# Four edits to a fused attention and Fourier-mixing kernel: spare products, raw weight places, two copies, the list of steps

## The chip, the cores and the metric

The kernel runs on one core of a Trainium2 chip. The metric is the device time of one execution in microseconds (us), lower being better; runs are given as a median with the lowest and the highest. The engines are TensorE (PE in the profile, with its weight loads as PEld), VectorE (DVE), ScalarE (ACT), GpSimd (POOL) and SyncE (SP), which issues most of the transfers. Each engine works through its own instructions in the order in which the program lists them.

## What is computed

For 4 batches of 8 heads, 768 tokens and head size 48, a gated linear attention; then, on the heads laid side by side (768 tokens by 384), a Fourier mixing block. Everything is f32.

```python
f = 1.0 / (1.0 + np.exp(-f_logit))
for t in range(S):
    state = f[:, :, t, :, None] * state + np.einsum('bhd,bhe->bhde', k[:, :, t], v[:, :, t])
    y[:, :, t] = np.einsum('bhd,bhde->bhe', q[:, :, t], state)
...
mixed = np.real(np.fft.fft(np.fft.fft(x, axis=1), axis=2))
u = x + mixed
un = (u - mean(u)) / np.sqrt(var(u) + 1e-06)
out = u + np.maximum(un @ w_ch1, 0.0) @ w_ch2
```

w_ch1 is 384 by 1536 and w_ch2 is 1536 by 384. They arrive as 64-bit floats, two 32-bit words per number, and the kernel makes f32 of them.

## The kernel before

**The order is written by hand.** The string ORDER holds 720 words; the kernel walks through them, and each word issues the next piece of one activity to the engines' queues. Nothing reorders the instructions afterwards, so the list sets the order on every engine, SP's and POOL's queues included.

- A number (0 to 15) is the next step of that attention unit. A unit is a pair of heads of one batch: units 0 to 3 are batch 0. Its steps, in order: exp and ln on ACT (L372, L373); a scan over the tokens on DVE (L379); three exps on ACT (L383, L384, L387); two multiplies on DVE (L391, L392); the score products on PE (L400); a masked copy on DVE (L404); products with v into the PSUM tile y (L559), the second score products (L576) and their copy to ao on ACT (L579); the rest of L559 and the state products (L599); a scan of the states on DVE (L607); the products of q with the states (L616) into y and five copies to yT on ACT (L625 to L629); transposes on PE (L636) and two copies to x on ACT (L640, L641); the fold of the tokens on DVE (L663 to L669); for units 2 and 3 of a batch also the sums over the channels (L678 to L687). There is one tile y, so the next unit's L559 waits for the yT copies of the one before it. K is the transpose of the keys (L538) and its copy to kT (L540).
- F is the next step of a batch's Fourier part: four z products (L725) with copies on ACT (L728 to L730), then three mix products (L744), whose sums go to x on DVE (L800, L803) with mean and variance (L766, L767). The first z needs the folds of all four units of the batch. H normalises a block of 128 tokens (L780), transposes it (L783) and copies it (L784).
- P is the next step of a batch's products with w_ch1 and w_ch2. Batch 0 goes through plain products (L872 up, L881 down); later batches use sums of blocks that save products (L841 up, L895 down). B makes one of the sums of w_ch1 (L813, L815), W the sums of w_ch2 (L358 to L361, in combine).
- C makes f32 of one block of weights (128 by 384): ACT scales the low words (L281), DVE shifts and masks the high words (L283, L284), POOL adds the two (L285). There are 24 blocks. r is the load of one block's raw words (L310) and R of three; V loads raw words again later and c looks at their sizes (L344).
- L loads the f, k, q or v of a unit (L206 to L213). I and Z set constants on POOL (I also the tile bound, which every scan reads), T and S load and sort the Fourier tables, i loads the identity, M joins the flags that decide whether a second, careful pass is needed.
- D is a group of spare products (L192): eight bf16 products of 128 by 128 of the tile bound with itself, into an unused part of y. Nobody reads them. There are 21 groups, all before F0.

**The raw words** lie in a pool tile with three places. A place is free again when POOL's addition (L285) of its block is done. The sums of w_ch2 (t2, t3, t4 in combine) use the same three places afterwards.

**The fold.** In L663 to L669 DVE makes sums and differences of mirrored tokens. Two of its seven instructions are plain copies: L667, f[:, 1:7:5] from f[:, 0:8:7] (128 x 192), and L668, one row f[0:1, 0] from f[0:1, 2] (1 x 96). The last one, L669, writes f[0:1, 2] and f[0:1, 6] and so must come after L668.

Of the kernel before, what the change touches and what calls it, by code (L numbers as in the profile page):

```python
# [7 lines left out]
F32 = mybir.dt.float32  # L8
U32 = mybir.dt.uint32
# [3 lines left out]
C = 128  # L13
# [11 lines left out]


ORDER = (
    "I L0f D L1f 0 D 0 1 L2f D D D D D L0q L0k D L1k 2 Z 0 D 1 i D D L1q L3q 0 0 0 L0v L3fk D 1 r 1 L2q D "
    "D L1v L2k 2 0 1 K0 3 0 0 D r 3 r D 2 0 1 1 2 C K1 L2v 1 2 1 C 3 2 C 1 K2 3 L4fk 4 2 r 1 2 L5fk D 4 5 "
    "L3v 1 3 2 D D T C 2 3 0 L4qv K3 5 3 0 2 3 D 3 2 3 S 2 3 D 3 L6fk 6 R 3 4 F0 5 F0 4 L5qv F0 C F0 5 "  # L30
    "L6qv K4 C r C 4 4 r F0 5 4 H0 H0 r C 4 H0 4 C L7fk r F0 r 7 F0 6 4 P0 C L7qv K5 P0 P0 r C r 5 C P0 r "
    "7 P0 5 6 4 6 P0 C C P0 5 K6 5 L8fk r C P0 7 7 P0 5 6 r P0 C 8 P0 r 6 r C P0 6 7 C K7 H0 C r 7 P0 r 6 "
    "C r 6 5 P0 C 6 H0 C P0 B 7 r C 6 r C 7 H0 L9fk L8qv P0 8 P0 P0 9 9 7 9 L9qv 6 P0 P0 P0 P0 9 7 9 K9 "
    "H0 P0 8 9 P0 P0 7 5 P0 P0 B P0 P0 8 7 B 9 8 4 9 H0 B W P0 P0 P0 9 P0 6 P0 P0 L11fk B P0 11 P0 P0 P0 "
    "P0 B B P0 11 9 8 K8 7 P0 P0 P0 11 8 F1 F1 F1 P0 P0 B L11qv F1 B P0 8 11 8 F1 11 8 L10fk P0 H1 B 10 B "
    "K11 P0 P0 P0 P0 L10qv 10 B 10 P0 10 P0 P0 10 H1 11 P0 P0 10 B B P0 B P0 H1 B P0 10 K10 P1 P1 P1 P1 "
    "P1 P1 P1 P1 L12fk P1 P1 P1 P1 P1 P1 F1 P1 F1 10 8 12 10 P1 8 12 10 12 9 P1 P1 P1 P1 L12qv 12 11 9 12 "
    "P1 H1 P1 H1 P1 12 11 K12 H1 H1 11 11 H1 L13fk P1 P1 P1 L13qv P1 P1 P1 P1 P1 P1 13 P1 P1 P1 P1 P1 13 "
    "P1 P1 12 10 P1 P1 13 13 12 10 12 11 P1 P1 P1 11 10 P1 L14fk 14 12 P1 K13 P1 11 F2 F2 P1 P1 14 P1 P1 "
    "L14qv P1 F2 P1 P1 14 P1 P1 P1 P1 P1 P1 14 F2 13 F2 P1 13 F2 P1 13 F2 P1 13 14 L15fk H2 15 13 14 13 "  # L40
    "K14 P1 15 L15qv 15 P1 P1 P1 14 15 H2 P1 H2 14 H2 P1 P2 14 P2 P2 P2 P2 P2 P2 P2 P2 P2 P2 P2 P2 P2 P2 "
    "13 14 15 K15 H2 H2 15 15 14 P2 V 15 H2 14 15 13 P2 14 c V 15 12 12 P2 P2 15 P2 15 V P2 P2 15 P2 F3 "
    "F3 F3 P2 H2 c V P2 P2 P2 V V P2 P2 P2 P2 P2 P2 P2 c P2 c c F3 P2 V F3 V F3 V c P2 P2 F3 P2 P2 P2 P2 "
    "P2 P2 H3 P2 H3 P2 V P2 P2 H3 P2 c P2 c c P2 P2 V P2 P2 P2 P2 P2 P2 P2 V P2 P2 P2 c c P2 c V V c V P2 "
    "V P2 P2 V P2 P2 H3 P3 c H3 P3 P3 P3 P3 P3 P3 P3 P3 P3 P3 P3 P3 c P2 P3 P3 H3 c P3 P3 P3 V P3 V P3 V "
    "c P3 P3 H3 P3 P3 H3 P3 c V P3 P3 P3 P3 P3 P3 P3 P3 V P3 P3 P3 P3 c P3 c P3 P3 P3 P3 P3 P3 P3 P3 P3 "
    "P3 V P3 c c P3 P3 P3 P3 P3 P3 c V P3 c P3 P3 P3 P3 P3 M P3 P3 P3 P3 P3 P3 P3 P3"
)


# [33 lines left out]
def kernel(  # L84
# [13 lines left out]
    nc = tc.nc  # L98
    B, HP, _, D, _, S = qkf.shape
    NCH = S // C  # L100
    DM = HP * 2 * D
    DFF = w_ch1.shape[1]
    NF = DFF // 128
    NQ = S // 4 + 1
    HS = S // 2
    HD = DM // 2
    QS, QD = S // 4, DM // 4
    R = 64 + D
# [9 lines left out]
    pr = ctx.enter_context(tc.tile_pool(name="pr", bufs=3))  # L118
# [7 lines left out]
    spare = y_out[:, 0, 3 * C:]  # L126

    def fixed(shape, tag):
        return const.tile(shape, F32, tag=tag, name=tag)
# [20 lines left out]
    bound = const.tile([128, S], mybir.dt.bfloat16, tag="bound", name="bound")  # L150
# [13 lines left out]
    eps = fixed([128, 1], "eps")  # L164
    two = fixed([128, 1], "two")
    small = fixed([128, 2 * NF], "small")

    place = const.tile([128, B, 4], U32, tag="place", name="place")

# [17 lines left out]
    started = []  # L187

    def busy():

        for _ in range(8):
            nc.tensor.matmul(spare, lhsT=bound[:, :C], rhs=bound[:, :C], start=not started, stop=True,  # L192
                             skip_group_check=True)
            started.append(True)

    v_of = {}
# [108 lines left out]

    def words(i):
        _, src, cols = blocks_of[i]
        raw = pr.tile([128, 2, 3, DM // 2], U32, tag="raw", name=f"raw{i}").rearrange("p a b n -> p (a b n)")
        raw = raw[:, :768].rearrange("p (n w) -> p n w", w=2)
        nc.sync.dma_start(out=raw.rearrange("p n w -> p (n w)"),  # L310
                          in_=src.bitcast(U32)[:, 2 * cols.start:2 * cols.stop])
        return raw

    def fetch(n=1):
        for _ in range(n):
            if wide and len(raws) < len(blocks_of):
                raws.append(words(len(raws)))
# [32 lines left out]
    def combine():  # L350

        H = NF // 2
        w11, w12, w21, w22 = [w2[:, i * H:(i + 1) * H, j * HD:(j + 1) * HD] for i in range(2) for j in range(2)]
        t2, t3, t4 = [pr.tile([128, H, HD], F32, tag="raw", name=f"block{i}") for i in range(3)]
        tt = nc.vector.tensor_tensor
        tt(t3, w22, w12, ALU.subtract)  # L358
        tt(w12, w12, w11, ALU.subtract)
        tt(t2, w22, w12, ALU.subtract)  # L360
        tt(t4, w21, t2, ALU.subtract)  # L361
        blocks[1], blocks[2], blocks[4] = w11, w21, t4
        blocks[5], blocks[6], blocks[3], blocks[7] = w12, t2, w22, t3
# [178 lines left out]
    def outputs(u, x_all, AT, Q, K, te, T=None):  # L542
# [98 lines left out]
        nc.scalar.copy(x_to[:, 3:], heads[:, 3:])  # L641
        yield
        yield from fold(u, x)

    eo_of = {}

    def fold(u, x):

        b, hp = divmod(u, HP)
        if b not in eo_of:
            eo_of[b] = p1.tile([128, 8, DM], F32, tag="eo", name=f"eo{b}")
        eo = eo_of[b]
        ch = slice(hp * 2 * D, (hp + 1) * 2 * D)
        f = eo[:, :, ch]  # L660
        last = hp == HP - 1
        tt = nc.vector.tensor_tensor
        tt(f[:, 6:3:-1], x[:, 0:3, ch], x[:, 3:6, ch], ALU.subtract)  # L663
        tt(f[:, 1:4], x[:, 0:3, ch], x[:, 3:6, ch], ALU.add)
        tt(f[:, 0:8:7], f[:, 1:7:5], f[:, 2:6:3], ALU.add)
        tt(f[:, 2:6:3], f[:, 1:7:5], f[:, 2:6:3], ALU.subtract)
        nc.vector.tensor_copy(f[:, 1:7:5], f[:, 0:8:7])  # L667
        nc.vector.tensor_copy(f[0:1, 0], f[0:1, 2])  # L668
        tt(f[0:1, 2:7:4], x[0:1, 0:2, ch], x[0:1, 3:5, ch], ALU.subtract)  # L669
        if hp < HP // 2:  # L670
            return
        yield


        lo, hi = (QD + 1, HD) if hp == HP // 2 else (1, QD + 1)
        up = slice(DM - lo, DM - hi, -1)
        tt = nc.vector.tensor_tensor
        tt(xs[:, :, lo:hi], eo[:, 4:7, lo:hi], eo[:, 4:7, up], ALU.subtract)  # L678
        if last:
            eo_of.pop(b)  # L680
            tt(se[:, :, 1:QD], xs[:, :, 1:QD], xs[:, :, HD - 1:QD:-1], ALU.subtract)
            tt(xs[:, :, 1:QD + 1], xs[:, :, 1:QD + 1], xs[:, :, HD - 1:QD - 1:-1], ALU.add)
        tt(xc[:, :, lo:hi], eo[:, 0:4, lo:hi], eo[:, 0:4, up], ALU.add)
        if last:
            nc.vector.tensor_copy(xc[:, :, 0:HD + 1:HD], eo[:, 0:4, 0:HD + 1:HD])
            tt(ce, xc[:, :, 0:QD + 1], xc[:, :, HD:QD - 1:-1], ALU.add)
            tt(xc[:, :, 0:QD], xc[:, :, 0:QD], xc[:, :, HD:QD:-1], ALU.subtract)  # L687
# [269 lines left out]
    with tc.manual_schedule():  # L957
        for word in ORDER.split():
            kind, n = word[0], int("0" + "".join(c for c in word if c.isdigit()))
# [10 lines left out]
            elif kind == "P":  # L970
                next(rest[n], None)
            elif kind == "W":
                combine()
            elif kind == "B":
                weight_sum()
# [31 lines left out]
    with tc.If(again > 0):  # L1007
        if wide:
            for i, (dst, _, _) in enumerate(blocks_of):
                single_or_zero(dst, words(i))  # L1010
        else:
            for i, (dst, src, cols) in enumerate(blocks_of):
                nc.sync.dma_start(out=dst, in_=src[:, cols])
        combine()
        nc.sync.dma_start(out=causal.rearrange("p (i n) -> p i n", n=32), in_=sel)
        for u in range(4):
            load(u, *("fkqv" if u < 3 else "qv"))
        for b in range(B):
            x = p2.tile([128, NCH, DM], F32, tag="x", name=f"again{b}")
            for hp in range(HP):  # L1020
                for _ in attention_by_blocks(b * HP + hp, lambda: x):
                    pass
            for _ in fnet(b, x):
                pass
            for _ in projected(b, x, again=True):
                pass
# [69 lines left out]
```

## Time and profile before

| | |
|---|---|
| median of 3 runs | 528.33 us (527.76 to 528.81) |
| the profiled execution | 527.43 us |
| its span, first to last instruction | 525.7 us |
| mean granted TensorE clock | 0.98 |
| busy PE / PEld / DVE / ACT / POOL | 94% / 86% / 72% / 41% / 12% |
| chain that ended last | PE 80%, DVE 9%, DMA 4%, issue 2%, ACT 2% |
| moved by DMA | 48.15 MB, mean 92 GB/s |

The busy shares are averages over the whole span. In the lines shown further on, a line of the timeline or of the chain begins with the start in us and the duration in us; behind it come engine, line of the kernel, operation, and what is written from what. A square bracket at the end gives how long the engine stood idle before the instruction and what released it. Where a line ends in x24, so many instructions are merged. An f32 product written once in the program shows as two records. The table by 10 us gives the busy time of each engine within the stretch, then the granted clock (1.00 is full speed), the share of the DMA engines and GB/s.

### The profile page before, as it was taken

Reading aid. Unit: us, or ns where it says so; the run is one execution under the profiler, and the core shown is the slowest. Engines: PE = TensorE matmul, PEld = TensorE weight load, DVE = VectorE, ACT = ScalarE, POOL = GpSimd, SP = SyncE. Lnnn points to the kernel's source line nnn. Section 1 sums busy time; section 2 is a strip of 40 time slices with the busy share of each in tenths; the row PEclk is TensorE's granted clock in tenths of the full one; section 3 lists DMA queues with packets and bytes.
Section 4 is the critical chain, followed back from the end, with each engine's and each line's share of the span. In section 5 each row is a group of like instructions: output and inputs, shape, how many; then the busy total and the mean of one; then the engine's idle time right before and its main releaser. Section 6 shows DMA issues by size and latency. Waiting matters only on the chain.

```text
span 525.7 us, 13813 instructions
## 1 busy us (share of the span) xinstructions
PE 494.9 (94%) x5854; PEld 452.8 (86%) x5854; DVE 378.6 (72%) x746; ACT 216.8 (41%) x520; POOL 61.3 (12%) x85
## 2 busy tenths in 40 slices
PE   6788699989999999999999999999999999999994
PEld 5676478756898889999999999998999999999994
DVE  4669999868986378588688696679586665565571
ACT  7484658753423351452543524341431404131220
POOL 3047034541002000000001000000001000010000
PEclk9879799999999999999999999999999999999998
DMA  8979476672002110222112012122140330410201
GB/s 222 277 192 268 98 198 187 184 215 85 28 28 85 54 56 28 57 55 86 54 56 84 1 55 73 46 62 68 53 122 15 107 135 1 136 61 1 92 2 36
DMA packets 20505, 48.15 MB, mean 92 GB/s; under 512 B 3409, under 2 KB 6034, under 8 KB 20434
## 3 DMA queue, kind: packets, MB, share of 16 engines
q1 hardware_dynamic: 19186, 43.43, 29.3%
q0 software_dynamic: 1104, 3.54, 1.8%
q8 instruction: 48, 0.79, 0.6%
q14 instruction: 23, 0.19, 0.1%
q10 hardware_dynamic: 144, 0.20, 0.1%
HBM read 42.44 MB, written 4.72 MB: 90 GB/s over the span
## 4 chain that ended last, share of the span: by engine, by line
PE 80%; DVE 9%; DMA 4%; issue 2%; ACT 2%; SPq 0%; POOL 0%; DVEq 0%; POOLq 0%; ACTq 0%
PE ub L841 23%; PE fx L895 16%; PE fz L895 12%; PE up L872 6%; PE z L725 4%; PE mix L744 3%; PE y L559 3%; PE po L881 2%; PE sc L400 2%; PE y L616 2%; DMA raw<-in_w_ch_dram 2%; PE pt L783 2%; PE ds L599 1%; PE st L538 1%; DVE W L379 1%
## 5 line engine op out<-in xcount | busy, mean ns | idle before, releaser
L850 DVE TENSOR_TENSOR h<-h,ub 128x512 f32<-128x512 f32 x81 | 55.6, 688 | 38.9 <-PE ub L841 27.2
L692 POOL DMA_INDIRECT out_dram<-x,place x16 | 17.7, 1107 | 383.7 <-DVE x L925 254.0
L848 ACT ACTIVATE h<-ub 128x512 f32<-128x512 f32 x54 | 32.0, 593 | 45.0 <-PE ub L841 45.0
L872 PE MATMUL up<-unT,w 128*128 128x256 f32 x216 | 50.0, 382 | 0.0
L841 PE MATMUL ub<-wide,w 128*128 128x128 f32 x360 | 45.2, 277 | 2.1 <-DVE wide L815 2.1
L895 PE MATMUL fx<-block,h 128*128 128x192 f32 x264 | 46.8, 327 | 0.0
L895 PE MATMUL fx<-w,h 128*128 128x192 f32 x264 | 45.6, 327 | 0.0
L872 PEld LDWEIGHTS up<-unT,w 128*128 128x128 f32 x216 | 39.8, 190 | 6.2 <-ACT h L874 0.9
L841 PEld LDWEIGHTS ub<-wide,w 128*128 128x128 f32 x360 | 42.4, 192 | 3.1 <-PE fx L895 1.2
L895 PEld LDWEIGHTS fx<-block,h 128*128 128x128 f32 x264 | 43.3, 190 | 0.4 <-DVE x L922 0.2
L852 ACT ACTIVATE h<-h 128x512 f32<-128x512 f32 x45 | 28.3, 630 | 36.9 <-DVE h L850 36.8
L895 PEld LDWEIGHTS fx<-w,h 128*128 128x128 f32 x264 | 42.8, 190 | 0.4 <-issue 0.2
L841 PE MATMUL ub<-unT,w 128*128 128x128 f32 x288 | 36.8, 275 | 0.0
L285 POOL TENSOR_TENSOR w<-w,raw 128x384 uint32<-128x384 uint32 x24 | 28.1, 1173 | 71.6 <-ACT raw L281 42.8
L841 PEld LDWEIGHTS ub<-unT,w 128*128 128x128 f32 x288 | 34.5, 192 | 0.1
L784 ACT COPY unT<-pt 128x384 f32<-128x384 f32 x24 | 11.4, 485 | 48.5 <-PE pt L783 48.5
L841 PE MATMUL ub<-unT,wide 128*128 128x128 f32 x216 | 29.1, 278 | 0.0
L841 PE MATMUL ub<-wide 128*128 128x128 f32 x216 | 28.6, 275 | 0.4 <-DVE wide L815 0.4
L379 DVE TENSOR_TENSOR_SCAN W<-g,bound 112x768 f32<-112x768 f32 x12 | 21.2, 1766 | 8.7 <-ACT g L373 8.7
L874 ACT ACTIVATE h<-up 128x256 f32<-128x256 f32 x36 | 13.8, 386 | 31.7 <-PE up L872 31.4
L841 PEld LDWEIGHTS ub<-unT,wide 128*128 128x128 f32 x216 | 26.4, 192 | 0.5
L841 PEld LDWEIGHTS ub<-wide 128*128 128x128 f32 x216 | 26.3, 192 | 0.5 <-PE ub L841 0.5
(189 smaller groups left out, 1001.6 us busy)
## 6 DMA issues: line engine op xcount, KB each, us to landing
raw<-in_w_ch_dram SPq DMA_DIRECT2D x24, 384.0 KB, 5.3
v<-in_v_dram SPq DMA_DIRECT2D x16, 288.0 KB
k<-in_w_ch_dram SPq DMA_DIRECT2D x12, 384.0 KB
g<-in_w_ch_dram SPq DMA_DIRECT2D x12, 384.0 KB, 3.5
k<-in_qkf_dram SPq DMA_DIRECT2D x14, 288.0 KB, 5.9
g<-in_qkf_dram SPq DMA_DIRECT2D x12, 288.0 KB, 5.6
q<-in_qkf_dram SPq DMA_DIRECT2D x12, 288.0 KB, 4.9
wide<-in_qkf_dram SPq DMA_DIRECT2D x10, 288.0 KB, 5.2
```

What stands on the lines that cost most here:

```text
L285: nc.gpsimd.tensor_tensor(bits, bits, lo, ALU.add)
L379: nc.vector.tensor_tensor_scan(W, g, bound[:R], 0.0, ALU.add, ALU.min)
L559: nc.tensor.matmul(y[FILL[g], c // 3, c % 3 * C + t.start:c % 3 * C + t.stop], lhsT=vals[rows, o:o + (64 if g == 0 else D)], rhs=weights, ...
L692: nc.gpsimd.indirect_dma_start(out=out.rearrange("b s d -> (b s) d"), out_offset=bass.IndirectOffsetOnAxis(ap=place[:, b, i:i + 1], axis=0 ...
L725: nc.tensor.matmul(z[:, cols], lhsT=src[:, j, lo:hi], rhs=tab[:, t, T % 2, cols], start=(i == 0), stop=(i == len(parts) - 1), skip_group_c ...
L744: nc.tensor.matmul(mix[:, o], lhsT=zz[:rows_of[T], T, PLACES[c]], rhs=cd[:rows_of[T], T, :NQ - odd], start=(i == 0), stop=(i == 1))
L841: nc.tensor.matmul(chains[chain][:, m * 128:(m + 1) * 128], lhsT=block(w)[:, m * 128:(m + 1) * 128], rhs=tokens(a), start=(new and m == 0) ...
L848: nc.scalar.activation(out, got, kind, scale=1.0 if how == "=+" else -1.0)
L850: nc.vector.tensor_tensor(out, out, got, ALU.add if how == "+" else ALU.subtract)
L852: nc.scalar.activation(out, out, AF.Relu)
L872: nc.tensor.matmul(pp[:, :256], lhsT=w1[:, kt, m * 128:(m + 1) * 128], rhs=unT[:, kt], start=(kt == 0), stop=(kt == 2))
L895: nc.tensor.matmul(out, lhsT=h[:, m], rhs=blocks[i][:, m], start=(start and m == 0), stop=(m == H - 1), skip_group_check=True)
```

## The change

1. **Spare products.** A group D becomes two f32 products of 128 by 128, on the words of bound read as f32, instead of eight bf16 ones.
2. **Raw words.** A fixed tile, ring, takes the place of the three pool tiles. It has the same size in all, 3456 words in each partition. Block i goes to place i % 4 of 768 words each, so that four fit; t2, t3 and t4 use the same tile.
3. **Fold.** The two copies, L667 and L668, go from DVE to ACT. L669 stays on DVE.
4. **The list.** ORDER holds the same words, each as often as before (720 in all, 21 of them D), in another order.

```diff
+    ring = fixed([128, 3 * NF // 2 * HD], "ring")
...
-        for _ in range(8):
-            nc.tensor.matmul(spare, lhsT=bound[:, :C], rhs=bound[:, :C], start=not started, stop=True,
-                             skip_group_check=True)
+        words = bound.bitcast(F32)[:, :C]
+        for _ in range(2):
+            nc.tensor.matmul(spare, lhsT=words, rhs=words, start=not started, stop=True, skip_group_check=True)
             started.append(True)
...
-        raw = pr.tile([128, 2, 3, DM // 2], U32, tag="raw", name=f"raw{i}").rearrange("p a b n -> p (a b n)")
-        raw = raw[:, :768].rearrange("p (n w) -> p n w", w=2)
+        raw = ring[:, i % 4 * 2 * DM:(i % 4 + 1) * 2 * DM].bitcast(U32).rearrange("p (n w) -> p n w", w=2)
...
-        t2, t3, t4 = [pr.tile([128, H, HD], F32, tag="raw", name=f"block{i}") for i in range(3)]
+        t2, t3, t4 = [ring[:, i * H * HD:(i + 1) * H * HD].rearrange("p (m n) -> p m n", m=H) for i in range(3)]
...
-        nc.vector.tensor_copy(f[:, 1:7:5], f[:, 0:8:7])
-        nc.vector.tensor_copy(f[0:1, 0], f[0:1, 2])
+        nc.scalar.copy(f[:, 1:7:5], f[:, 0:8:7])
+        nc.scalar.copy(f[0:1, 0], f[0:1, 2])
```

The list up to the first F0, before and after (the rest is interleaved anew in the same way):

```
before
I L0f D L1f 0 D 0 1 L2f D D D D D L0q L0k D L1k 2 Z 0 D 1 i D D L1q L3q 0 0 0 L0v L3fk D 1 r 1 L2q D
D L1v L2k 2 0 1 K0 3 0 0 D r 3 r D 2 0 1 1 2 C K1 L2v 1 2 1 C 3 2 C 1 K2 3 L4fk 4 2 r 1 2 L5fk D 4 5
L3v 1 3 2 D D T C 2 3 0 L4qv K3 5 3 0 2 3 D 3 2 3 S 2 3 D 3 L6fk 6 R 3 4 F0
after
L2q Z I L0f D D L1f i 0 D L2f L0k D L0q D D L1k 1 D L0v D D 0 D 2 L3q D 0 0 1 D 0 K0 1 0 D 0 L1q 1 r
L3fk D 1 L2v L2k 3 2 C 1 0 L1v r 0 D 2 D 0 K1 2 K2 3 1 1 L5fk L3v 2 L4fk C 1 T 2 3 3 1 r 5 1 D r D 5
2 4 3 S 1 2 D L6fk 2 3 4 2 0 K3 3 L5qv 0 D 3 3 2 3 C 2 3 3 2 5 3 D 4 F0
```

In the new list, ahead of F0, three weight blocks are made instead of four; unit 0's multiplies come before unit 1's scan; the channel sums of unit 2 come after the fold of unit 3 instead of before it; and the table sort S comes earlier. Behind the first F0, the seventh and last F0 comes after eight P0 instead of before the first one; W stands directly ahead of unit 5's fold and unit 8's multiplies, where before three P0 followed it.

## The prediction

> **What bounds the kernel now.** I read the slices of the page first, then the table of busy time by 10 us, then the chain that ended last within the first 125 us, then the timeline where that chain waits.
>
> ```profile
> PE   6788699989999999999999999999999999999994
> DVE  4669999868986378588688696679586665565571
> PEclk9879799999999999999999999999999999999998
> ```
>
> Each digit stands for 13.1 us. From the fifth slice on PE shows almost nothing but nines; before that it has holes, and only there does the granted clock fall. DVE is full in slices 4 to 8 and then loosens. The table by 10 us (PE, PEld, DVE, ACT, POOL busy; clock; DMA share) says it in numbers:
>
> ```profile
> 50.00:60.00 10.00, 4.53 (x40) 3.34 (x41) 9.21 (x25) 5.38 (x13) 2.73 (x4) 0.72 0.83 218
> 80.00:90.00 10.00, 10.00 (x146) 8.07 (x146) 9.69 (x15) 8.25 (x20) 4.39 (x3) 1.00 0.60 159
> 110.00:120.00 10.00, 8.12 (x140) 5.59 (x139) 4.81 (x9) 5.24 (x11) 3.16 (x3) 1.00 0.66 183
> 420.00:430.00 10.00, 10.00 (x64) 10.00 (x63) 6.70 (x13) 0.00 (x0) 0.00 (x0) 1.00 0.46 157
> ```
>
> So the end is set by two things: when PE gets its first Fourier product (the z of F0, L725), and what PE waits after it. All four attention units of batch 0 must be folded before that z. The PE work listed ahead of F0 (units 0 to 3, 21 spare groups) and behind it is the same in both lists; only its order differs. Hence: shift of the end = shift of the first z + change of PE's waits behind it. The chain shows the two places:
>
> ```profile
> 53.69 3.93 issue
> 57.62 2.86 PE z L725 x6
> 109.37 5.48 DMA raw<-in_w_ch_dram
> ```
>
> PE stands 3.93 us and then starts z at 57.62. The timeline tells for what: DVE's folds of units 2 and 3 run in one row without a gap over 0.24 us, and L681, which makes se for that z, runs 57.05 to 57.51.
>
> ```profile
> 55.26 0.36 DVE L666 TENSOR_TENSOR eo<-eo 128x192 f32<-128x192 f32 x1
> 55.65 0.26 DVE L667 COPY eo<-eo 128x192 f32<-128x192 f32 x1
> 55.95 0.20 DVE L668 COPY eo<-eo 1x96 f32<-1x96 f32 x1
> 56.18 0.35 DVE L669 TENSOR_TENSOR eo<-x 1x192 f32<-1x192 f32 x1
> ```
>
> The second place is the raw weight words:
>
> ```profile
> SPq L310 <- POOL w L285: 41.8, 18, 10.2
> 114.87 0.36 DVE L283 TENSOR_SCALAR w<-raw 128x384 uint32<-128x384 uint32 x1 [2.55 <-DMA raw<-in_w_ch_dram]
> 116.28 0.55 PE L783 MATMUL pt<-ident,un 128*128 128x128 f32 x3 [1.88 <-DVE un L780]
> ```
>
> SP held 18 raw loads back for 41.8 us until POOL had freed one of three places; at 114.87 DVE therefore waited 2.55 us, and the normalised rows (L780) queued behind it made PE wait 1.88 us.
>
> **Part 1, spare products.** A group was eight bf16 products and becomes two f32 ones; an f32 product shows as two records (fx and fz: 462 written, 924 recorded). At full clock 16 bf16 records took 1.00 us in the chain, so 0.50 us a group; 112 f32 records of the same 128 columns (L841) took 12.76 us, so four take 0.46 us. 21 groups: about 0.9 us less PE time, all of it in stretches where PE waits for something else: 0. If the fold row no longer covers it, it is a gain of at most 0.9. The clock is the other bound: one half-clock window is 3.4 us long (40 slices, clock rows) and costs at most 1.7 us, either way.
>
> **Part 2, two fold copies.** On DVE L667 and L668 take 0.53 us a fold (55.65 to 56.18); 16 folds, 8.5 us of DVE. But L669 overwrites what the second copy reads, so DVE now waits there for ACT, with nothing in between. Nearest ACT rows: 96x192 copy (L728) 0.316, 112x4 copy (L629) 0.202, hand-offs 0.03 (ACT to DVE, L383 to L391) to 0.09 (L373 to L379); three of them give 0.65 to 0.75, I take 0.69 for L666's end to L669's start against 0.56 now. So with ACT free the move loses 0.13 us a fold. With ACT busy it loses up to what ACT has ahead of the copies: in the new list an exp/ln pair of 1.9 us for unit 1, kT and ao (0.63 + 0.48) for unit 0, one raw conversion (0.66) for unit 2, x copies for unit 3. Behind L669 on DVE wait the state scans (L607), and PE and the next unit wait for those; behind the copies on ACT wait the yT copies that free y. In the PE-bound part twelve folds lie beside at least 0.3 of idle DVE: 0 there, but the combination of w2 (L358 to L361, 5.4 us) is now followed directly by a fold and by unit 8's products: from unit 9's L392 on DVE has 15.4 us of rows before PE may do unit 8's L400, PE has 13.5; +0 to +2.4, I take 0, because DVE arrives earlier there (part 3).
>
> [...]
>
> **Part 3, four raw places.** From POOL's release to the next use of a place: load 3.7 to 5.5 us (chain), ACT and DVE about 1.2, POOL 1.1: some 6 us or more. Three places give a block each 2.0 us, four each 1.5. DVE waited 3.7 us in all for raw words (three times), PE 2.1 us around 114 to 116 (start to start 2.13, of which 0.1 is work). I take 2.1; bounds 0 and 3.7.
>
> **Part 4, the list up to the first z.** By rows of before, in the new queue orders (times in us):
>
> ```
>                               before   after, worked out
> first exp on ACT               4.44     5.4   q of unit 2 is issued first: 2 x 0.46
> unit 0 L400 on PE             12.5     13.4
> unit 1's scan ends            10.0     15.1   now behind unit 0's L391, L392
> unit 0 L607                   21.7     22.0   gap of 3.25 before it now filled
> unit 1's first L559           27.0     25.6
> unit 1 L607                   31.8     29.8
> fifth scan (L379) starts      37.8     34.5   one weight block fewer before it
> unit 2 L607                   42.1     39.4
> unit 3's L616 ends            51.3     49.2
> se ready                      57.5     57.0
> ```
>
> The list gains 3.3 us by the fifth scan. It gives most of it back: unit 1's fold copies stand behind an exp/ln pair (-0.6), unit 3's x copies behind a conversion and unit 2's fold copies (-1.2), and unit 2's L678 and L683 (0.45 + 0.55), formerly in the gap before unit 3's fold, now lie on the row to se. z: -0.6; bounds -3.5 (lead kept) and +4.
>
> Behind z, the first up products (L872) are listed ahead of the last mix step instead of after it. DVE has 15 us of rows from se to the second normalisation (L780) that they need, against 19.7 from se to the first L872 (77.2) in before. PE had one real hole there, 1.44 us at 69.8; I take half of it, -0.7, bounds -1.4 and +1.4. From then on both lists have the same steps, interleaved nearly alike; 0.
>
> **Sum.** -0.6 - 2.1 - 0.7 = -3.4 us. The profiled execution took 527.43 (span 525.7 and 1.7 around it): 524.0. The median of the runs is 0.9 above the profiled one, 528.33: **524.9**.
>
> **Rivals.**
> 1. *The lead of the list is kept* (ACT is free when the folds come): z -3.5 instead of -0.6: 522.0. For it: ACT is busy 5.4 of 10 us at 50 to 60. Against: 9.7 of 10 at 30 to 40.
> 2. *The raw words were hidden anyway*: PE shows 10.00 of 10 from 80 to 100, DVE 9.7; with DVE's work unchanged another of its rows is late at 114, and the up products only move. Parts 3 and 4 behind z give 0: 527.7, no difference.
> 3. *The wait takes the copies' place, slower*: DVE at L669 waits out one exp/ln pair of ACT (1.9 us) in each of the four folds before z: +7.6 there instead of -0.6, 533.1. It decides from 0.85 us of extra wait a fold (3.4 / 4), that is when L666's end to L669's start is over 1.5 us on average of four. For it: both engines run strictly in the listed order, and ACT was late by 1.4 us at 8 to 9.6 already for such a pair (L383 behind unit 2's). Against: in the new list only unit 1 has a pair there.
>
> **Chances.** Forecast 0.50, rival 1 0.15, rival 2 0.13, rival 3 0.22. A difference of 0.2% (1.06 us) is about what can be told from none. Faster 0.65, same 0.13, slower 0.22. Range: down to all good bounds, -3.5 - 3.7 - 1.4 = -8.6, 519.7; up, to half of rival 3's loss, as beyond it less than 1 in 10 is left: 531.
>
> **What would show it.** z's start: 55 to 58.5 supports part 4, beyond 60 rival 3. L666's end to L669's start: 0.7 for a free ACT. DVE's and ACT's waits for raw words between 95 and 120: near 0 if part 3 holds; PE's hole at its pt there gone. SP's wait for POOL at L310 well under 41.8. Spare groups of 0.46 us and an unchanged number of half-clock windows. I'm wrong if PE's waits behind 120 us, where I book 0, move by more than 2 us.

## The result and the profile after

The changed kernel takes **531.29 us** (528.69 to 534.44, 20 runs) where the kernel before takes 528.32 (527.42 to 531.83, 20 runs) beside it. The ratio is 1.0052, 95% interval 1.0035 to 1.0069: slower by about half a per cent, above the forecast of 524.9 and 0.3 us over the upper end of its range. The profiled execution took 533.2 us (span 531.5, mean granted clock 0.977). It is 1.9 us above its median, and that of before 0.9 us below its own; so the two traces differ by 5.8 us where the medians differ by 3.0. Below, times within a trace come from these two; what a part costs comes from the medians of the experiments.

From L167 to L306 the line numbers of the changed kernel are one higher (L213 is L212 of before, L282 is L281, L284 to L286 are L283 to L285); the fold keeps L663 to L669. The raw words are now called ring.

The slices of the page of the changed kernel, 13.3 us each:

```profile
PE   5787599899999999999999999999999999999994
...
PEclk9897699999999999999999999999999999999998
```

PE shows almost only nines from the sixth slice on, as before. In the fifth (53 to 66 us), where the Fourier products start, PE went from 6 to 5 and the granted clock from 7 to 6. The table of busy time by 10 us (PE, PEld, DVE, ACT, POOL; granted clock; DMA share; GB/s) of the changed kernel reads:

```profile
50.00:60.00 10.00, 4.33 (x103) 3.52 (x93) 7.11 (x18) 5.61 (x18) 1.01 (x1) 0.81 1.03 282
...
80.00:90.00 10.00, 10.00 (x243) 8.53 (x242) 9.70 (x16) 8.28 (x19) 3.50 (x4) 1.00 0.66 193
110.00:120.00 10.00, 9.28 (x146) 6.32 (x145) 9.83 (x14) 7.56 (x15) 6.00 (x6) 1.00 0.53 156
```

From 50 to 60 DVE is busy 7.11 of 10 us instead of 9.21, although it works on the same folds: the two waits at L669 take 1.53 us of it, and the folds come later. PE's row at 110 to 120 improved from 8.12 to 9.28. The chain that ended last, in the changed kernel, has in place of the start of z at 57.62:

```profile
55.44 0.54 DVE eo L669
55.97 4.58 issue
60.55 8.38 PE z L725 x28
```

The first z starts 2.93 us later than before. The timeline of DVE in the changed kernel shows the folds of units 1 and 3 (start, duration; the bracket is the idle time before the instruction and what ended it):

```profile
39.28 0.36 DVE L666 TENSOR_TENSOR eo<-eo 128x192 f32<-128x192 f32 x1
42.58 0.34 DVE L669 TENSOR_TENSOR eo<-x 1x192 f32<-1x192 f32 x1 [2.94 <-ACT eo L668]
42.86 0.74 DVE L607 TENSOR_TENSOR_SCAN stt<-ds,te 112x288 f32<-112x288 f32 x1
...
58.41 0.35 DVE L669 TENSOR_TENSOR eo<-x 1x192 f32<-1x192 f32 x1 [0.72 <-ACT eo L668]
```

With ACT free the hand-over takes 0.72 us from L666's end to L669's start, against 0.56 with both copies on DVE. In the four folds ahead of z it is 0.72, 0.81, 1.08 and, for unit 1, 2.94. Directly behind that L669 on DVE stands unit 2's state scan L607, for which PE waits. The same stretch on ACT:

```profile
37.11 0.48 ACT L579 COPY ao<-sc 128x384 f32<-128x384 f32 x1 [0.40 <-PE sc L576]
40.20 0.84 ACT L372 ACTIVATE g<-g 112x768 f32<-112x768 f32 x1 [2.60 <-DMA g<-in_qkf_dram]
...
41.91 0.34 ACT L667 COPY eo<-eo 128x192 f32<-128x192 f32 x1
42.28 0.27 ACT L668 COPY eo<-eo 1x96 f32<-1x96 f32 x1
```

ACT was idle when L666 ended at 39.64. It could not take the copies, because unit 4's exp and ln stood ahead of them in its queue, and the exp waited 2.60 us for its f. The timeline of SP says why f was late:

```profile
21.28 0.48 SPq L310 DMA_DIRECT2D ring<-in_w_ch_dram  x1
28.88 0.33 SPq L213 DMA_DIRECT2D g<-in_qkf_dram  x1
...
32.50 0.58 SPq L213 DMA_DIRECT2D g<-in_qkf_dram  x1
```

Between 20 and 34 us the waits of SP's queue show what it waited for:

```profile
SPq L213 <- PE sc L576: 6.9, 1, 6.9
```

SP stood from 21.8 to 28.9 at the load of unit 5's f (28.88), whose place unit 1's L576 was still reading; unit 4's f comes behind it in the list, at 32.50, and was there for the exp 7.7 us later, at 40.20. A chain over four engines: SP held by PE, f late by SP, ACT held by f, DVE held by ACT. In before the fold was on DVE alone, and neither the exp nor the load could hold it.

The waits of the changed kernel, in all, with the number of times and the longest:

```profile
ACT eo L667 <- DVE eo L666: 17.5, 9, 4.9
DVE eo L669 <- ACT eo L668: 15.6, 16, 2.9
...
SPq L310 <- POOL w L286: 23.9, 14, 2.8
```

Each hand-over can hold both engines: DVE waited 15.6 us at L669, and ACT stood still for 17.5 us with the copies at its head while DVE was not yet there. Of the 15.6 us, 8.5 is time in which DVE itself made the copies before (16 folds of 0.53 us). What of these sums costs time is for the experiments to tell. SP's wait for POOL fell from 41.8 to 23.9 us.

Behind z, PE's waits of over 0.4 us sum to 8.02 us against 6.45 before. With z's 2.93 that is 4.5 of the 5.8 us between the traces; a further 1.2 is the clock: z's products ran at half clock for 5.9 us from their start (until 66.5), before for 3.6 (until 61.2), and half of the difference is lost (in before's trace six z products take 2.85 us at half clock, and six others, of one column more, 1.54 at 367 us, where the clock is 1.00).

### The profile page after: what moved, and what is told of

The parts are those of the page before. It is cut to its first block, busy times and chain, and to the rows that moved or that the text cites. A ratio compares the mean times of both kernels' runs of the same rounds, so it can differ in the third digit from the quotient of the medians.

```text
span 531.5 us, 13640 instructions
## 1 busy us (share of the span) xinstructions
PE 494.9 (93%) x5770; PEld 453.6 (85%) x5770; DVE 371.5 (70%) x714; ACT 226.6 (43%) x552; POOL 57.0 (11%) x85
## 4 chain that ended last, share of the span: by engine, by line
PE 79%; DVE 8%; DMA 6%; ACT 3%; issue 2%; SPq 1%; DVEq 0%; ACTq 0%
PE ub L841 23%; PE fx L895 16%; PE fz L895 12%; PE up L872 5%; PE z L725 5%; PE y L559 3%; PE po L881 3%; PE mix L744 2%; DMA g<-in_qkf_dram 2%; DMA wide<-in_qkf_dram 2%; PE y L616 2%; PE ds L599 2%; PE pt L783 2%; DVE w L285 1%; PE yt L636 1%
## 5 line engine op out<-in xcount | busy, mean ns | idle before, releaser
L895 PE MATMUL fx<-ring,h 128*128 128x192 f32 x264 | 46.6, 327 | 0.0
L895 PEld LDWEIGHTS fx<-ring,h 128*128 128x128 f32 x264 | 43.3, 190 | 0.1
L286 POOL TENSOR_TENSOR w<-w,ring 128x384 uint32<-128x384 uint32 x24 | 27.0, 1131 | 70.3 <-ACT ring L282 30.2
L784 ACT COPY unT<-pt 128x384 f32<-128x384 f32 x24 | 11.7, 490 | 43.1 <-PE pt L783 43.0
L770 ACT ACTIVATE rstd<-mv,eps 128x1 f32<-128x1 f32 (+1 forms) x20 | 5.9, 294 | 43.1 <-DVE mv L767 43.1
```

What stands on the lines that cost most here:

```text
L286: nc.gpsimd.tensor_tensor(bits, bits, lo, ALU.add)
L895: nc.tensor.matmul(out, lhsT=h[:, m], rhs=blocks[i][:, m], start=(start and m == 0), stop=(m == H - 1), skip_group_check=True)
```

## The experiments

Three theories at first. **A:** the copies on ACT cost the time, because L669 waits behind whatever ACT's queue holds. **B:** the new list itself delays z, with its late opening and late f, whoever makes the copies. **C:** the spare products in f32 words cost the time. Later runs narrow A, as their texts say. Every run was timed in the same batch as the kernel before; ratios are to it.

### The spare products alone

```diff
-        for _ in range(8):
-            nc.tensor.matmul(spare, lhsT=bound[:, :C], rhs=bound[:, :C], start=not started, stop=True,
+        words = bound.bitcast(F32)[:, :C]
+        for _ in range(2):
+            nc.tensor.matmul(spare, lhsT=words, rhs=words, start=not started, stop=True, skip_group_check=True)
```

> Before, with only the spare products changed (two f32 products a group instead of eight bf16). [...] Theory C (the spare products cost it, because they alter the clock of TensorE ahead of the first z) expects 530 or more and more half-clock time than the 17 us of before.

Measured: 528.44 us, ratio 0.9995 (0.9965 to 1.0024); first z at 57.31 instead of 57.62, and 17.1 us at half clock in both traces (without the stretch behind PE's last row, 3.6 us in before's trace). No effect that can be measured; C falls.

### The four places alone

```diff
-        raw = pr.tile([128, 2, 3, DM // 2], U32, tag="raw", name=f"raw{i}").rearrange("p a b n -> p (a b n)")
+        raw = ring[:, i % 4 * 2 * DM:(i % 4 + 1) * 2 * DM].bitcast(U32).rearrange("p (n w) -> p n w", w=2)
```

> Before, with only the ring of four places for the raw words; copies on VectorE, bf16 spares, the old list. The prediction's part 3 expects -2.1 us (526.2), bounds 0 to -3.7, with no wait of VectorE for raw words between 95 and 120 us. The rival (the transfers were hidden anyway: in the changed kernel VectorE had no such wait, but its L285 took 1.26 instead of 0.56 us in 8 of 24 blocks instead of 4, those that ran beside the addition on GpSimd) expects 528.3 within 1 us, with the 2.13 us hole of TensorE at 114 us replaced by others.

Measured: 526.8 us, ratio 0.9976 (0.9952 to 1.0000). PE's hole of 1.88 us at 116 is gone, and its waits of over 0.4 us behind z fall from 6.45 to 4.57. With the old list the fourth place is worth about 1.7 us, with an interval that reaches from 2.5 to 0. In this trace z starts at 59.09, 1.47 us later than in before's, although the list is the same; the trace has 23.9 us at half clock, counted in the same way, before's 17.1.

### The copies on ACT alone, old list

```diff
-        nc.vector.tensor_copy(f[:, 1:7:5], f[:, 0:8:7])
-        nc.vector.tensor_copy(f[0:1, 0], f[0:1, 2])
+        nc.scalar.copy(f[:, 1:7:5], f[:, 0:8:7])
+        nc.scalar.copy(f[0:1, 0], f[0:1, 2])
```

> Before, with only the two fold copies on ScalarE, old list. Theory A expects it slower: in the old list too ScalarE has work queued ahead of the copies (for unit 1 an exp/ln pair, for unit 3 an exp/ln pair of unit 6), so the first z starts 2 to 5 us later and the time is 530 to 533. Theory B expects no difference beyond 4 x 0.13 us: 528.3 to 529.

Measured: 534.46 us, ratio 1.0122 (1.0087 to 1.0158): with the old list the two copies cost about 6 us, more than the whole change and more than A expected. Nor are the waits where A put them, in the folds ahead of z. Fourteen of sixteen folds show the 0.72 us of a free ACT. The sixth and the thirteenth show 4.11 and 2.79. ACT's and DVE's timelines of this kernel at the sixth:

```profile
134.07 0.83 ACT L383 ACTIVATE g<-W 112x768 f32<-112x768 f32 x1
...
136.07 0.69 ACT L874 ACTIVATE h<-up 128x256 f32<-128x256 f32 x2
...
137.54 0.36 ACT L667 COPY eo<-eo 128x192 f32<-128x192 f32 x1
```

```profile
138.24 0.35 DVE L669 TENSOR_TENSOR eo<-x 1x192 f32<-1x192 f32 x1 [4.11 <-ACT eo L668]
```

L666 ended at 134.12; three exps of unit 8, two h copies and unit 7's x copies were listed ahead of unit 5's fold. Ahead of z no L669 waited long, and yet z came 1.84 us late (59.46). There the other side of the hand-over shows, on ACT:

```profile
52.33 0.35 ACT L667 COPY eo<-eo 128x192 f32<-128x192 f32 x1 [2.22 <-DVE eo L666]
...
52.89 0.35 ACT L625 COPY yT<-y 112x254 f32<-112x254 f32 x1
```

ACT stood 2.22 us at unit 2's fold with unit 3's yT copies behind it; they began at 52.89 instead of 51.35, 1.16 us after the products that they copy had ended (51.73), where before it was 0.05. Behind z PE's waits of over 0.4 us sum to 8.64 us instead of 6.45.

### The change with the copies back on DVE

```diff
-        nc.scalar.copy(f[:, 1:7:5], f[:, 0:8:7])
-        nc.scalar.copy(f[0:1, 0], f[0:1, 2])
+        nc.vector.tensor_copy(f[:, 1:7:5], f[:, 0:8:7])
+        nc.vector.tensor_copy(f[0:1, 0], f[0:1, 2])
```

> The changed kernel with the two copies back on VectorE. Theory A: the four waits of L669 ahead of the first z (2.94, 1.08, 0.81, 0.72 us) go and 4 x 0.53 us of copies come back, so z starts at 57 to 58 instead of 60.5 and the time is about 528, 3 us under the changed kernel. Theory B: z starts no earlier than 59.5, since the f of unit 4 lands at 40 us in any case and unit 4's scan follows in the row; the time is 530 to 531.

Measured: 528.13 us, ratio 0.9994 (0.9971 to 1.0016); first z at 56.49. So in the new list the copies cost 3.2 us, all of the loss and a little more: A holds, and B, which expected 530 to 531, falls. But this kernel has the fourth place as well, and is not faster than before. In its trace z starts 1.1 us earlier than before, and PE's waits behind z sum to 7.53 us, 1.1 more than before and 3.0 more than with the old list and four places. That the list by itself starts z earlier is not shown by one trace, as the run with the old list behind z shows below.

### One word moved: unit 4's exp behind unit 1's fold

The changed kernel, copies on ACT, with the word "4" of the first step (exp and ln) put directly after unit 1's fold, which is the "1" behind S:

```diff
-5 1 D r D 5 2 4 3 S 1 2 D L6fk 2 3 4 2 0 K3 3
+5 1 D r D 5 2 3 S 1 4 2 D L6fk 2 3 4 2 0 K3 3
```

> The changed kernel (copies on ScalarE) with one word moved: the first step of unit 4 (exp and ln) comes after unit 1's fold instead of before it. If what costs is the work queued on ScalarE ahead of the copies, the wait of 2.94 us before L669 falls to the 0.72 us of a free ScalarE and the time to 529 to 529.5. If it is mostly the other side, ScalarE standing still at L667 until VectorE gets there (17.5 us in all in the changed kernel) and the 0.16 us that each hand-off is longer than the two copies were, the time stays within 1 us of the changed kernel, 530.3 to 532.3.

Measured: 528.62 us, ratio 0.9999 (0.9978 to 1.0019): one word takes back 2.7 of the 3.0 us, a little more than expected. First z at 55.89; unit 1's gap is 0.72. ACT's timeline of this kernel:

```profile
39.14 0.35 ACT L667 COPY eo<-eo 128x192 f32<-128x192 f32 x1 [2.09 <-DVE eo L666]
...
40.19 0.84 ACT L372 ACTIVATE g<-g 112x768 f32<-112x768 f32 x1 [0.40 <-DMA g<-in_qkf_dram]
```

The f is as late as before (40.19), and nobody waits for it now but its own exp. The load was not the fault by itself; what stood behind its user was. ACT still stands at L667 until DVE arrives, 20.8 us in all here against 17.5 in the changed kernel, and the time is shorter all the same: that sum is not what cost the 2.7 us. Two things stay open. The changed kernel with the load alone put right was not tried. And these 12 runs had a mean granted clock of 0.983, those of the changed kernel 0.980, which is 18 against 21 us at half clock (2 x (1 - clock) x the span); as at most about half of such time is lost (in before's trace six z products take 2.85 us at half clock, six others 1.54 at full), up to 1.6 of the 2.7 us may, as an estimate, have come by way of the clock (up to 1.3 of the 3.2 with the copies on DVE, clock 0.982).

### The new list up to z, the old one behind it

Copies on DVE, four places, f32 words; the new words up to the first F0, then the rest in the old order (which has one C, one step of unit 6 and loads ahead of F0).

```diff
 ... 2 3 3 2 5 3 D 4
-F0 6 5 F0 L4qv F0 R F0 C L6qv 4 C 4 C 4 F0 4 L7fk K4 ...
+C L4qv 6 R F0 F0 4 F0 C F0 5 L6qv K4 C r C 4 4 r F0 5 4 H0 H0 ...
```

> Copies on VectorE, four places, f32 spares; the new list up to the first z, from there the old list's order. In e4 (new list throughout) the first z started at 56.5 against 57.6 before, but TensorE then had four holes of 1.17, 0.52, 1.50 and 0.93 us up to 110 us, where the old list with four places (e2) has one of 1.44. If the new list's rest is what eats its early lead, the time is 2 to 2.7 us under e4's 528.1: 525.4 to 526.1. If the holes only move, it is 528 within 1 us.

Measured: 527.49 us, ratio 0.9977 (0.9956 to 0.9998). Only 0.6 us better than the new rest (528.13), within the noise of both. With the old rest PE waits 1.13 us at 70.16 and 2.16 at 73.24: the holes move rather than go.

Up to the sums that make se, DVE works through the same instructions here as with the new rest, and yet the first z of the two traces lies 1.18 us apart. With the new rest, then with the old one:

```profile
56.49 2.85 PE L725 MATMUL z<-tab,se 128*95 128x385 f32 x6 [5.13 <-issue]
```

```profile
57.67 2.85 PE L725 MATMUL z<-tab,se 128*95 128x385 f32 x6 [5.01 <-issue]
```

The stretches of half clock (3.4 or 6.8 us long in before's trace, 3.4, 6.8 and 10.2 in the changed kernel's) lie elsewhere: from 15.9 to 22.7 us and from 50.0 in the first trace, from 23.7 to 27.1 and from 54.5 in the second. With the old list z varies as much (57.62 before, 59.09 with four places). So the start of z in a single trace is uncertain by more than 1 us, and a lead of that size is not shown by it.

### Unit 4's f loaded ahead of unit 5's

As the run before, with "L4fk" listed before "L5fk":

```diff
-2 K2 3 1 1 L5fk L3v 2 L4fk C 1 T
+2 K2 3 1 1 L4fk L5fk L3v 2 C 1 T
```

> e7 with the load of unit 4's f and k put ahead of that of unit 5 in the load queue. In the changed kernel SP stood from 21.8 to 28.9 us at unit 5's f, whose place unit 1 still used, and unit 4's f landed only at 40.2. If that hold matters, the first z comes 1 to 2 us earlier than in e7 and the time is 1 to 2 us under e7's. If not (the scan of unit 4 is not on the row to the z), it equals e7 within 1 us.

Measured: 527.29 us, ratio 0.9975 (0.9951 to 0.9999), the same as the run before. The load was on time here (unit 4's exp starts at 39.61 without a wait for it, in the run before at 41.86 after 3.90 us): with the copies on DVE a late f for unit 4 costs nothing that can be measured.

### The old opening

As the run two before, but with the tile bound set first, and q of unit 2 and Z at their later places:

```diff
-L2q Z I L0f D D L1f i 0 D L2f L0k D L0q D D L1k 1 D L0v
+I L0f D D L1f i 0 D L2f L0k D L0q D D L1k Z 1 D L0v
...
-L1q 1 r
+L1q L2q 1 r
```

> e7 with the old opening: constants of the tile bound first, unit 0's f as the first load, unit 2's q after unit 1's. The first f landed at 6.5 us in the changed kernel and at 4.4 before. If the late opening is passed on to the first z, it comes 1 to 2 us earlier than in e7 and the time is 1 to 2 us less; if unit 0 to 2 wait for later loads in any case, it equals e7 within 1 us.

Measured: 529.91 us, ratio 1.0026 (1.0001 to 1.0051): 2.4 us worse than the new opening, although the first exp starts at 4.63 instead of 5.96; z starts at 58.59 instead of 57.67. Both expectations failed: an early first exp is not what sets z here. The clock points at a reason: the mean granted clock of the 12 runs is 0.972, with the new opening 0.980, which is 29 against 21 us at half clock. Whether the opening brings this about, and by which of the moved loads, was not tried.

### Old list, copies on ACT, four words moved, with its control

```diff
-3.stt 2.FOLD 3.y,yT          (steps by unit and name, in the order of the list)
+3.stt 3.y,yT 2.FOLD
...
-8.exps 9.masked P0 P0 7.x 5.FOLD P0
+9.masked P0 P0 5.FOLD 8.exps 7.x P0
...
-H2 14.FOLD
+14.FOLD H2
```

> The kernel before with the two fold copies on ScalarE and four words of the old list moved: unit 2's fold comes after unit 3's yT copies; unit 8's exps and unit 7's x copies come after unit 5's fold; the transpose copy of H2 comes after unit 14's fold. With the old list unmoved the copies cost 6.1 us (534.46), with L666-to-L669 gaps of 4.11 us in the sixth fold and 2.79 us in the thirteenth. Theory A (the cost is the order of ScalarE's queue around the copies): both gaps fall to about 0.7 us and the time to 528 to 530 us. Theory B (each hand-off between VectorE and ScalarE costs its time, whatever stands in the queue): 533 us or more.

> The same four words moved, but the fold copies stay on VectorE: the control for what the moved words do by themselves. Theory A and theory B both expect 528 to 529 us (no change against the kernel before); if it is faster than 527 us or slower than 530 us, the moved words have a price of their own that must be taken off the other run.

Measured: 532.38 us on ACT (ratio 1.0083, 1.0054 to 1.0112), 529.22 on DVE (1.0012, 0.9986 to 1.0037). The pair differs by 3.2 us where the old list's pair differed by 6.0. 532.38 lies between what A and B expected, and the trace says why. The thirteenth fold went to 0.72. At the sixth the copies now stand ahead of the exps, but also behind three steps of P0, and ACT's and DVE's timelines of the kernel with the copies on ACT read:

```profile
133.66 0.38 ACT L874 ACTIVATE h<-up 128x256 f32<-128x256 f32 x1 [0.91 <-PE up L872]
134.95 0.39 ACT L874 ACTIVATE h<-up 128x256 f32<-128x256 f32 x1 [0.91 <-PE up L872]
135.23 0.34 ACT L667 COPY eo<-eo 128x192 f32<-128x192 f32 x1
```

```profile
135.91 0.34 DVE L669 TENSOR_TENSOR eo<-x 1x192 f32<-1x192 f32 x1 [3.20 <-ACT eo L668]
...
142.66 0.35 DVE L669 TENSOR_TENSOR eo<-x 1x192 f32<-1x192 f32 x1 [2.35 <-ACT eo L668]
```

ACT was mostly idle, but each h copy waits for its up product, and PE delivers one every 1.29 us; the fold copies wait with them. Behind it PE waited 0.71 and 1.81 us that its control does not have. Up to 131.7 us the trace with the copies on ACT is 0.43 us ahead of its control, at 145 it is 2.02 behind, and it stays so: in these traces the pair's difference is made at these two folds.

### The same two folds ahead of the h copies, with its control

```diff
-H0 P0 9.masked P0 P0 5.FOLD 8.exps 7.x P0 P0 B P0 P0 8.MUL 7.FOLD
+H0 5.FOLD P0 9.masked P0 P0 8.exps 7.x P0 7.FOLD P0 B P0 P0 8.MUL
```

> As the run before it with copies on ScalarE and four words moved (532.38), but units 5's and 7's folds are listed ahead of the up-product steps whose ReLU copies (three h of L874 that PE paces at 1.29 us each) stood ahead of the fold copies there: unit 5's fold directly after H0's transpose copy, unit 7's after the next up step. Theory A (queue order): the gaps of 3.20 and 2.35 us at the sixth and seventh fold fall below 1 us, PE's holes of 0.71 and 1.81 us behind them go, and the time falls by 1.9 to 2.5 us to about 530. Theory B (the hand-offs themselves): 532 or more.

> The same list with the copies on VectorE, the control: theory A expects the run with copies on ScalarE to be within 1.3 us of this one (16 folds, of which the four before the first z lose 0.16 us each, and some ScalarE standing still); theory B expects a difference of 3 us as in the pair before. By itself about 529, as the control before it.

Measured: 532.07 us on ACT (1.0066, 1.0045 to 1.0087), 530.99 on DVE (1.0051, 1.0026 to 1.0076). The pair differs by 1.1 us, as A expected; the gaps are 1.93 (A said below 1; the copies stood behind kT, L540, and H0's copy, L784) and 0.72. The time did not fall to 530, because the moved folds cost about 1.8 us on DVE too (there PE waits 1.07 us at an L400 that it did not wait for in the control before). So the order that suits the copies on ACT is not the order that suits the rest.

The pairs together, ACT minus DVE with the same list:

```
list                                    DVE      ACT     difference
old                                     528.5    534.5      6.0
old, four words moved                   529.2    532.4      3.2
old, two more folds moved               531.0    532.1      1.1
new (the change)                        528.1    531.3      3.2
new, unit 4's exp behind unit 1's fold  (528.1)  528.6      0.5
```

The two copies are the same in every row; only what stands around them in the queues differs. (In the last row the DVE value is that of the unmoved list, and rows come from different batches, whose own before lies between 528.2 and 528.6. By the intervals of the ratios each difference is uncertain by 1.5 to 2 us, so that 1.1 and 0.5 cannot be told from 0, while 3.2 and 6.0 can.)

## Why the prediction was wrong

The forecast was 6.4 us too low (524.9 against 531.29), in two parts of like size. With the copies back on DVE the rest of the change takes 528.13: 3.2 us are the copies, which the first item explains, and 3.2 us are gains of the list and the places that did not come, which the item on what lies behind z explains as far as it is known.

- **The step that failed** is in parts 2 and 4: "unit 1's fold copies stand behind an exp/ln pair (-0.6)", with 0.69 us from L666's end to L669's start for a free ACT. The free hand-over was right (0.72). The pair was counted as work of 1.9 us that would be partly over; it was read as busy time, and its own wait was not followed. In the trace the exp began 0.56 us after L666 had ended, since its f landed only at 40.20, and L669 waited 2.94 us. The f was late by a step that part 4 did not work out: SP stood 7 us at the load listed ahead of it. With the exp behind the fold, by one word, the loss goes (531.29 to 528.62). That the lateness of the load, and not the 1.9 us of work, made most of the wait is read from the trace.
- **Rival 3 had the mechanism** (the wait at L669 takes the copies' place) but not its shape. It asked for over 1.5 us on average of four folds; the average was 1.39, with one fold holding more than half of it. The start of z at 60.55 lay beyond the 60 us that the prediction gave as this rival's sign. The rival said nothing of ACT standing still at L667, which in the old list made the larger part of the loss ahead of z (1.1 of 1.84 us, at the yT copies); the sum of 17.5 us in the changed kernel is no measure of a loss, as the run with one word moved shows. Its price, 533.1, was 1.8 us too high.
- **Part 4, the row to z.** Against the worked-out column: first exp 6.51 (5.4), unit 0 L400 14.55 (13.4), unit 0 L607 23.82 (22.0), fifth scan 36.16 (34.5), unit 2 L607 42.86 (39.4), unit 3's L616 ended 53.2 (49.2), se ready 60.45 (57.0). The first 1.1 us were lost in the opening: f of unit 0 landed at 6.51, behind q of unit 2. The run with the old opening was slower, so taking that lateness away did not help. The next 1.8 came at unit 1's fold. With the copies on DVE z began at 56.49, and with one word moved at 55.89, earlier than before's 57.62; but with the same words ahead of it z began at 57.67 in another trace, so the gain forecast for the list (-0.6) is neither shown nor refuted.
- **Behind z, -0.7 and then 0.** Wrong in sign, and the second step that failed: PE's holes of before were taken off (here and in part 3), and no new ones were booked, as "both lists have the same steps, interleaved nearly alike; 0". The old list with four places waits 4.57 us there, the new list 7.53 (copies on DVE). Behind 120 us, where 0 was booked, PE's waits of over 0.4 us went from 3.35 us before to 5.00 in the changed kernel. In the changed kernel PE waits 0.91 us at 74.11 and 1.39 at 102.24 for ao (L579), and ACT's timeline shows ao behind H's rstd (L770), which waits for DVE:

```profile
101.01 0.30 ACT L770 ACTIVATE rstd<-mv,eps 128x1 f32<-128x1 f32 x1 [2.54 <-DVE mv L767]
...
101.71 0.47 ACT L579 COPY ao<-sc 128x384 f32<-128x384 f32 x1
```

  It is the same pattern as at the fold, at a place where the prediction looked at DVE's rows only. That this order alone makes the holes is read from the trace and was not tried by itself; with the old rest the time fell by only 0.6 us, within the noise. Its cause stays open.
- **Part 1, 0:** right (0.9995). The number of half-clock windows, given as a sign, stayed the same with the f32 words alone (17.1 us, five times 3.4); the changed kernel's trace has 20.5 us, six times 3.4 (both without the end of the span).
- **Part 3, -2.1:** right in size with the old list (-1.7, with an interval that includes 0; its hole of 1.88 is gone). In the new list DVE's and ACT's waits for raw words between 95 and 120 us are gone too, and PE's hole at L783 is 0.72 instead of 1.88; but the holes at L559 came in its place, so it does not show in the sum.
- **Part 2's DVE gain** in the later folds, taken as 0: the wait at L669 was mostly short there in the new list (one gap of 1.78, the others 0.72 to 0.95). The old list's later folds show that this was the list's doing: 4.11 and 2.79.
- The two prices: for a copy of 128x192 and one of 1x96 I took 0.316 and 0.202 us from the nearest rows, a 96x192 copy of z (L728) and a 112x4 copy of y (L629). ACT took 0.34 and 0.27 us, so these rows were too low a price. It is 0.1 us a fold and decided nothing.

In sum: f32 words 0; four places -1.7; the new list about +1.3 (528.13 against 526.8 in the same batch, with an interval that includes 0); the copies +3.2. Three kernels share the best ratios, 0.9975 to 0.9977, and cannot be told apart; the smallest edit among them is before with four places, 526.8 us, ratio 0.9976 (0.9952 to 1.0000).

## What to carry to other kernels

A small instruction moved to an engine with spare time inherits that engine's queue: price it not by busy shares, but by what stands ahead of it and what *that* waits for, back to the load, and price the instructions behind it as well, since the new engine now stands still until the old one arrives (17.5 us in all in the changed kernel). In a chain DVE, ACT, DVE the two copies took 0.16 us more at best, and 1.8 to 3.6 us more where an exp with a late load, other exps or copies paced by PE were listed ahead (gaps of 2.35 to 4.11 us instead of 0.56). A list of steps tuned around one placing of an operation has to be tuned again when the operation changes its engine. And no run here turned an earlier first z into a time clearly under that of four places alone: what the order behind it lets through counts as well.

## What the runs showed that I had not expected

- A DVE instruction more than doubled beside POOL: L285 (scalar_tensor_tensor with two inputs, 128x384) takes 0.56 us, but about 1.26 (1.25 to 1.39) when it starts while POOL's addition L286 runs. In the changed kernel DVE and POOL at 86 us:

```profile
86.63 1.26 DVE L285 SCALAR_TENSOR_TENSOR w<-ring,w 128x384 uint32<-128x384 uint32 x1
```

```profile
86.46 1.01 POOL L286 TENSOR_TENSOR w<-w,ring 128x384 uint32<-128x384 uint32 x1 [0.94 <-ACT h L874]
```

  8 of 24 blocks are so long in the changed kernel (19.1 us in all), 4 of 24 in before and in before with four places (16.2): the new list lays the two side by side more often, at 2.9 us of DVE. In each of the eight, L285 ends 0.41 to 0.43 us after POOL's addition does (87.89 and 87.47 in these rows), and none of the 16 short ones starts while POOL is at an addition. Why L285 is held up, the rows do not say.
- A first exp later by 1.3 us went with an end earlier by 2.4 (the old opening's run). The opening is not a row of its own: with it the clock of the runs changed as well (0.980 against 0.972).
- One execution of the same kernel differs from another by up to 5.8 us (528.69 to 534.44 for the changed kernel). The time goes with the clock: the four fastest of the 20 (528.7 to 529.3) had a mean granted clock of 0.983 to 0.985, the four slowest (532.9 to 534.4) 0.974 to 0.979. Here the two profiles alone would have told of a difference of 5.8 us, twice what the medians show.
